# A cross-attention block and a maxout MLP on one core: all loads as nine transfers on one queue, the state read in 128x32 array tiles, layer 1 by column halves

## The chip, the cores and the metric

The kernel runs on one core of one Trainium2 chip. The metric is the device time of one execution in microseconds, the median of several runs. A profile is one such execution recorded by the hardware; its span is some 2 us shorter than the device time of the same run. Engines are named as in the profile: PE (TensorE matmul), PEld (its weight loads), DVE (VectorE), ACT (ScalarE), POOL (GpSimd), SP (the sync engine, which here only issues DMA).

## The reference

For 8 batches of 8 heads, `x` (512 x 64 per head) reads from a `state` (32 x 64 per head) and the state reads from `x`; both results go through a maxout MLP.

```python
scores = scale * x @ state.T ;  xread = softmax(scores) @ state        # 512 rows a batch
scores2 = scale * state @ x.T ; sread = softmax(scores2) @ x           # 32 rows a batch
t = concat([xread, sread])      # (8*544, 512) over all heads
out = maximum(t @ w1, t @ w2) @ w_out      # w1, w2: 512x1024, w_out: 1024x512
```

Both kernels compute max(a, b) as b + relu(a - b). So they need w1 - w2 (the "weight subtraction", into `wcat[:, :, 0:1024]`), and w2 times w_out (into `wcat[:, :, 1024:1536]`, here "the product"). They never form xread: the state is multiplied by the weights first (`u_sw`, "state times weights"), then by the attention.

## The kernel before

The parts that the change touches, with cuts marked. In the traces here each engine takes up its work in the order of the program: x of batch 0 was cast by 12.5 us in this kernel, but its transposes wait behind those of the state until 21.4.

```python
for b in range(B):                                  # state: 8 pieces of 64 KB, ACT queue
    nc.scalar.dma_start(out=s_f[32 * (b % 4):32 * (b % 4) + 32, b // 4, :]..., in_=state[b]...)
load_x(0); load_x(1)                                # two transfers of 512 KB each, SP queue
for i in range(4):                                  # weights: 8 row blocks of 512 KB, SP queue
    nc.sync.dma_start(out=w2f[:, i, :], in_=moe_w2[128 * i:128 * i + 128])
    nc.sync.dma_start(out=w1f[:, i, :], in_=moe_w1[128 * i:128 * i + 128])
...
def u_sr(b, g):                                     # state read: E^T x, whole array
    for c in range(NC):
        nc.tensor.matmul(p[:, 0:257], d["e"][:, c, 4*g:4*g+4, :]..., d["xb"][:, c, g, 0:257], ...)
    nc.vector.reciprocal(d["rr"][:, g:g + 1], p[:, 256:257])
    nc.vector.tensor_scalar(d["sr"][:, :, g, :], p[:, 0:256]..., scalar1=d["rr"][:, g:g + 1], ...)
...
cast_x(0, ("V", "A"))
states(0)                                           # state transposes, batches 0 to 3
states(1)                                           # the same for batches 4 to 7
cast_x(1)
for b in range(2):
    for u in att_units(b):                          # attention of batches 0 and 1
        u()
for i in range(4):
    w_t(i)                                          # transposes of w2; subtractions beside them
    ...
u_sw(0, 0); u_sw(0, 1)
l1(0, ...); l1(1, {})                               # layer 1 of batches 0 and 1
for i in range(4):
    w_wo(i)                                         # the product of w2 and w_out
...
l2(0, {... attention of batch 2 ...})               # from here one batch after another
```

The softmax here doesn't subtract the row's maximum and nothing guards it: scores larger than these inputs give would overflow.

## Time and profile before

| | before |
|---|---|
| device time, median (range) of 4 runs | 196.72 us (194.87 to 197.77) |
| span of the profiled run | 195.7 us |
| PE busy | 162.1 us, 83% |
| first layer 1 matmul | 48.6 us |
| layer 2 of batch 0 starts | 66.2 us |
| one batch in the steady part | 16.7 us |

The steady part is nearly pure matmul time, so a change helps either by starting it earlier or by taking PE work out of it. The lines are in the prediction. One caution on reading them: the clock column of that run says 1.00 all through, yet its transposes at 21 us are 107 ns apart and those at 68 us 56 ns. The spacing of equal instructions is the better witness of the clock; the clock record of that run is not complete.

### The profile page before, as it was taken

The numbers are of one execution on the slowest core, as the hardware profiler recorded it, in microseconds if no ns is written. First come the engines' busy times: TensorE is split into PE (matmuls) and PEld (weight loads), VectorE is DVE, ScalarE is ACT, GpSimd is POOL, SyncE is SP. The second block draws the span as 40 slices with busy tenths as digits, with TensorE's granted clock in tenths as the row PEclk, the third lists the DMA queues.
The fourth block names the chain that finished last, engine by engine and source line by source line (L and its number), as shares of the span: only waits on it lengthen the run. The fifth ranks groups of instructions, "written<-read, shape, count | busy, mean of one in ns | idle before, by whom it ended". The sixth has DMA issues, their size and how long they took to land.

```text
span 195.7 us, 2920 instructions
## 1 busy us (share of the span) xinstructions
PE 162.1 (83%) x1192; PEld 84.1 (43%) x1192; DVE 92.1 (47%) x171; ACT 71.2 (36%) x123; POOL 36.4 (19%) x48
## 2 busy tenths in 40 slices
PE   0020688646999899999999999999999999999992
PEld 0010556432344356556445544545544544474440
DVE  1120465737670236466763584475277554232510
ACT  0050324264653351344811822562280261232311
POOL 1010540940000008043260071026004000000000
PEclk9999999999999999999999999999999999999999
DMA  5999970093000000943900750390050050052222
GB/s 166 323 343 381 376 233 3 0 165 50 0 3 0 0 0 5 281 150 121 302 9 3 229 199 3 139 290 2 3 214 0 3 214 0 0 218 54 55 107 107
DMA packets 14797, 23.25 MB, mean 119 GB/s; under 512 B 2880, under 2 KB 12096, under 8 KB 13888
## 3 DMA queue, kind: packets, MB, share of 16 engines
q1 hardware_dynamic: 11568, 21.50, 32.4%
q0 software_dynamic: 1040, 1.05, 3.5%
q10 hardware_dynamic: 2176, 0.52, 1.3%
q8 instruction: 9, 0.15, 0.3%
q14 instruction: 4, 0.03, 0.1%
HBM read 15.20 MB, written 8.91 MB: 123 GB/s over the span
## 4 chain that ended last, share of the span: by engine, by line
PE 67%; DMA 9%; ACT 9%; DVE 8%; issue 3%; POOL 2%; ACTq 1%; DVEq 0%; POOLq 0%
PE ps L249 26%; PE ps L234 11%; DMA s_f<-in_state_dram 9%; PE ps L247 7%; PE ps L144 4%; PE ps L291 4%; DVE es L163 3%; PE ps L210 3%; PE ps L175 3%; DVE r L225 2%; PE ps L186 2%; ACT xt L58 2%; PE ps L285 2%; POOL a L165 2%; ACT e L162 2%
## 5 line engine op out<-in xcount | busy, mean ns | idle before, releaser
L249 PE MATMUL ps<-wo,r 128*128 128x512 bf16 x256 | 61.2, 379 | 0.8 <-DVE r L225 0.8
L249 PEld LDWEIGHTS <-r 128*128 128x128 bf16 x256 | 25.0, 98 | 32.5 <-DVE r L225 2.8
L165 POOL TENSOR_TENSOR a<-e,er 128x512 bf16<-128x512 bf16 x16 | 16.6, 1046 | 94.5 <-DVE er L164 94.5
L234 PE MATMUL ps<-aT,sw 128*128 128x512 bf16 x128 | 33.5, 388 | 0.0
L58 ACT COPY ob<-ps 128x512 f32<-128x512 f32 x16 | 9.4, 585 | 58.7 <-PE ps L249 58.7
L225 DVE TENSOR_SCALAR r<-ps 128x512 bf16<-128x512 f32 x32 | 21.6, 674 | 10.0 <-PE ps L234 9.8
L223 ACT ACTIVATE r<-ps 128x512 bf16<-128x512 f32 x32 | 19.3, 604 | 6.3 <-PE ps L234 6.3
L60 DVE CAST sw<-ps 128x512 bf16<-128x512 f32 x24 | 16.2, 679 | 9.2 <-PE ps L210 9.1
L247 PE MATMUL ps<-sw,aT 128*128 128x512 bf16 x64 | 19.2, 381 | 0.6 <-DVE sw L60 0.6
L60 DVE COPY ob<-ps 128x512 f32<-128x512 f32 x16 | 10.9, 684 | 16.7 <-PE ps L249 16.7
L110 PE MATMUL ps<-ident,s_bf 128*128 128x128 bf16 x8 | 1.2, 308 | 19.5 <-DVE s_bf L60 19.5
L58 ACT CAST sw<-ps 128x512 bf16<-128x512 f32 x24 | 14.0, 589 | 7.2 <-PE ps L210 7.2
L163 DVE TENSOR_REDUCE es<-e 128x16 f32<-128x512 bf16 x16 | 10.7, 667 | 12.3 <-ACT e L162 12.3
L234 PEld LDWEIGHTS <-sw 128*128 128x128 bf16 x128 | 11.0, 100 | 11.0 <-issue 2.9
L62 POOL CAST xb<-xf 128x1024 bf16<-128x1024 f32 x14 | 15.1, 1107 | 0.0
L210 PE MATMUL ps<-wcat,st 64*32 64x512 bf16 x192 | 10.9, 405 | 0.7 <-DVE wcat L326 0.4
L175 PE MATMUL ps<-xb,e 128*128 128x257 bf16 x64 | 11.1, 308 | 0.4 <-ACT e L162 0.4
L58 ACT COPY xt<-ps 128x1024 bf16<-128x1024 bf16 x8 | 8.1, 1010 | 8.4 <-PE ps L144 5.4
L144 PE MATMUL ps<-ident,xb 128*128 128x128 bf16 x128 | 10.8, 243 | 0.0
L144 PEld LDWEIGHTS <-xb 128*128 128x128 bf16 x128 | 9.7, 111 | 2.4
L162 ACT ACTIVATE e<-ps 128x512 bf16<-128x512 f32 x16 | 9.6, 611 | 0.4 <-PE ps L158 0.4
L60 DVE COPY xt<-ps 128x1024 bf16<-128x1024 bf16 x8 | 5.5, 688 | 8.7 <-PE ps L144 8.7
(55 smaller groups left out, 133.5 us busy)
## 6 DMA issues: line engine op xcount, KB each, us to landing
xf<-in_x_dram SPq DMA_DIRECT2D x16, 512.0 KB, 7.1
out_dram<-ob SPq DMA_DIRECT2D x7, 1024.0 KB, 5.1
w2f<-in_moe_w_dram SPq DMA_DIRECT2D x4, 512.0 KB, 6.5
w1f<-in_moe_w_dram SPq DMA_DIRECT2D x4, 512.0 KB, 7.1
wo<-in_moe_w_out_dram POOLq DMA_DIRECT2D x1, 1024.0 KB, 9.5
out_dram<-ob SPq DMA_DIRECT2D x4, 256.0 KB, 2.0
s_f<-in_state_dram ACTq DMA_DIRECT2D x8, 64.0 KB, 7.4
out_dram<-obs SPq DMA_DIRECT2D x8, 64.0 KB, 1.7
```

What stands on the lines that cost most here:

```text
L58: nc.scalar.copy(o, i)
L60: nc.vector.tensor_copy(o, i)
L144: nc.tensor.transpose(p[:, (cc * 4 + k) * 128:(cc * 4 + k + 1) * 128], d["xb"][:, c, k // 2, (k % 2) * 128:(k % 2) * 128 + 128], ident)
L163: nc.vector.tensor_reduce(d["es"][:, sl], d["e"][:, sl], axis=mybir.AxisListType.X, op=ALU.add)
L165: nc.gpsimd.tensor_mul(d["a"][:, sl], d["e"][:, sl], d["er"][:, sl].unsqueeze(3).to_broadcast([128, 2, H, Ns]))
L175: nc.tensor.matmul(p[:, 0:257], d["e"][:, c, 4 * g:4 * g + 4, :].rearrange("p i n -> p (i n)"), d["xb"][:, c, g, 0:257], start=(c == 0), s ...
L210: nc.tensor.matmul(pg[g][32 * i:32 * i + 32, :], st2[64 * g:64 * g + 64, i, b * Ns:(b + 1) * Ns], wcat[64 * g:64 * g + 64, i, ch * 512:(ch ...
L223: nc.scalar.activation(out=o, in_=p, func=ACTF.Relu)
L225: nc.vector.tensor_scalar(o, p, scalar1=0.0, scalar2=None, op0=ALU.max)
L234: nc.tensor.matmul(p, SW[b][:, g, f * 128:(f + 1) * 128], AT[b][:, g, :], start=(g == 0), stop=(g == 1))
L247: nc.tensor.matmul(p, AT[b][:, g, cs], SW[b][:, g, FF:WC], start=(g == 0), stop=False)
L249: nc.tensor.matmul(p, r[:, f, cs], wo[:, f, :], start=False, stop=(f == NF - 1))
```

## The change

Its intent: get the loads out of the way with few large transfers, in the order of need; make the state read cheaper; begin layer 1 as soon as half the weight columns are there. The core of the diff:

```diff
-    for b in range(B):
-        nc.scalar.dma_start(out=s_f[32 * (b % 4):..., b // 4, :]..., in_=state[b]...)
+    nc.sync.dma_start(out=s_f, in_=state.rearrange("b (q h) n d -> (h n) (b q) d", q=2))
     load_x(0)                      # now one transfer each
     load_x(1)
-    for i in range(4):
-        nc.sync.dma_start(out=w2f[:, i, :], in_=moe_w2[128 * i:128 * i + 128])
-        nc.sync.dma_start(out=w1f[:, i, :], in_=moe_w1[128 * i:128 * i + 128])
+    for ch in range(2):
+        cs = slice(ch * 512, (ch + 1) * 512)
+        nc.sync.dma_start(out=w2f[:, :, cs], in_=moe_w2...[:, :, cs])
+        nc.sync.dma_start(out=w1f[:, :, cs], in_=moe_w1...[:, :, cs])
+    load_x(2)
+    nc.sync.dma_start(out=wof, in_=moe_w_out...)        # was a casting DMA of POOL

-    def u_sr(b, g):                       # 2 x 4 matmuls of 257 columns, 2 evictions of 256
+    def u_sr(b):                          # 32 matmuls of 65 columns, one eviction of 128
         for c in range(NC):
+            for g in range(2):
+                for i in range(4):
+                    nc.tensor.matmul(p[32*i:32*i+32, g*65:g*65+65], d["e"][:, c, 2*i+g, :],
+                                     d["xb"][:, c, i, 1+65*g:66+65*g], ...)
     def u_srt(b):                         # 4 transposes -> 1

-    states(0); states(1); cast_x(1); att(0); att(1); w_t; subtractions
-    u_sw(0, 0); u_sw(0, 1); l1(0); l1(1); w_wo; ...; l2(0, {attention of 2})
+    warm_up(12)                           # dummy matmuls
+    states(0)
+    cast_x(0, ("V", "A", "V", "P"))       # in quarters
+    u0[0:4]; cast_x(1); u1[0], u1[1], u0[5], u1[2], u1[3], u0[4]     # 0 and 1 interleaved
+    states(1)
+    u0[6], u1[4], u1[5]; w_sub(0); u_sw(0, 0); u_sw(1, 0)
+    l1(0, first half); l1(1, first half)
+    w_sub(1); u2[0], u2[1]; u_sw(0, 1); u_sw(1, 1)
+    l1(0, second half, {u2[2], u2[3]}); l1(1, second half)
+    w_t; casts of w_out on V, A, P; u2[4:7]; w_wo; ...; l2(0, {attention of 3})
```

Here `u0[k]`, `u1[k]`, `u2[k]` are the pieces of the attention of batches 0, 1 and 2: 0 and 1 transpose x, 2 and 3 make scores and exponentials, 4 is the state read, 5 transposes the attention, 6 the state read. A "128x32 tile" is a matmul that writes 32 of the 128 output partitions; the state read's four tiles write one strip each. V, A, P name the engines DVE, ACT, POOL.

More of the change, by code (lines that the diff above doesn't have):

```diff
@@ L62, in copy, with run @@
             nc.gpsimd.tensor_copy(o, i)
-    ident = consts.tile([128, 128], BF16)
-    make_identity(nc, ident)
+    def run(*units):
+        for u in units:
+            u()
     xf_t = {}
     def load_x(b):
-        xf = xio.tile([128, 2, 4, NC * D], F32, tag="xf", name="xf")
-        xf_t[b] = xf
-        for g in range(2):
-            nc.sync.dma_start(
-                out=xf[:, g, :, :],
-                in_=x[b].rearrange("(i g) (p c) d -> g p i (c d)", g=2, c=NC)[g],
-            )
-    s_f = stage.tile([128, B // 4, DM], F32)
-    for b in range(B):
-        nc.scalar.dma_start(
-            out=s_f[32 * (b % 4):32 * (b % 4) + 32, b // 4, :].rearrange("n (h d) -> n h d", h=H),
-            in_=state[b].rearrange("h n d -> n h d"),
-        )
+        xf_t[b] = xio.tile([128, H, NC * D], F32, tag="xf", name="xf")
+        nc.sync.dma_start(out=xf_t[b], in_=x[b].rearrange("h (p c) d -> p h (c d)", c=NC))
+    s_f = stage.tile([128, 2 * B, D], F32)
+    nc.sync.dma_start(out=s_f, in_=state.rearrange("b (q h) n d -> (h n) (b q) d", q=2))
     load_x(0)
@@ L88 @@
     w1f = stage.tile([128, 4, FF], F32)
-    for i in range(4):
-        nc.sync.dma_start(out=w2f[:, i, :], in_=moe_w2[128 * i:128 * i + 128])
-        nc.sync.dma_start(out=w1f[:, i, :], in_=moe_w1[128 * i:128 * i + 128])
+    wof = stage.tile([128, NF, DM], F32)
+    for ch in range(2):
+        cs = slice(ch * 512, (ch + 1) * 512)
+        nc.sync.dma_start(out=w2f[:, :, cs], in_=moe_w2.rearrange("(i p) f -> p i f", p=128)[:, :, cs])
+        nc.sync.dma_start(out=w1f[:, :, cs], in_=moe_w1.rearrange("(i p) f -> p i f", p=128)[:, :, cs])
+    load_x(2)
+    nc.sync.dma_start(out=wof, in_=moe_w_out.rearrange("(k p) n -> p k n", p=128))
+    ident = consts.tile([128, 128], BF16)
+    warm = consts.tile([128, 512], BF16)
+    nc.gpsimd.memset(warm, 0.0)
+    make_identity(nc, ident)
+    sbd = consts.tile([128, B, 4, 2, Ns], BF16)
+    nc.vector.memset(sbd, 0.0)
     wo = consts.tile([128, NF, DM], BF16)
@@ L96, with warm_up, states @@
     w2t = stage.tile([128, 4, NF, 128], BF16)
-    s_bf = stage.tile([128, B // 4, DM], BF16)
-    s_b2 = stage.tile([128, B // 4, 4, 2, D], BF16)
-    sbd = consts.tile([128, B, 4, 2 * Ns], BF16)
-    nc.vector.memset(sbd, 0.0)
-    st2 = consts.tile([128, 4, B * Ns], BF16)
-    def states(bb):
-        copy("V", s_bf[:, bb].rearrange("p (g i d) -> p g i d", g=2, i=4),
-             s_f[:, bb, :].rearrange("p (i g d) -> p g i d", g=2, i=4))
-        p = bank(BF16)
-        for k in range(4):
-            nc.tensor.transpose(p[:, k * 128:(k + 1) * 128], s_bf[:, bb, k * 128:(k + 1) * 128], ident)
-        for jj in range(2):
-            copy("A" if jj else "V",
-                 sbd[64 * jj:64 * jj + 64, 4 * bb:4 * bb + 4, :, 32 * jj:32 * jj + 32],
-                 p[64 * jj:64 * jj + 64, 0:512].rearrange("p (k b n) -> p b k n", k=4, b=4))
-        copy("P", s_b2[:, bb], s_f[:, bb, :].rearrange("p (i g d) -> p i g d", g=2, i=4))
-        p = bank(BF16)
-        for i in range(4):
-            nc.tensor.transpose(p[:, i * 128:(i + 1) * 128], s_b2[:, bb, i].rearrange("p g d -> p (g d)"), ident)
-        copy("V", st2[:, :, 128 * bb:128 * bb + 128],
-             p[:, 0:512].rearrange("p (i t) -> p i t", i=4))
+    def warm_up(n):
+        p = bank()
+        for k in range(n):
+            nc.tensor.matmul(p, warm[:, 0:128], warm, start=(k == 0), stop=(k == n - 1))
+    s_bf = stage.tile([128, 2 * B, 2, D], BF16)
+    def states(hb):
+        qs = slice(B * hb, B * hb + B)
+        copy("V", s_bf[:, qs], s_f[:, qs].unsqueeze(2).to_broadcast([128, B, 2, D]))
+        p = bank(BF16)
+        for q in range(B):
+            nc.tensor.transpose(p[:, q * 128:(q + 1) * 128], s_bf[:, B * hb + q].rearrange("p u d -> p (u d)"), ident)
+        for g in range(2):
+            copy("A" if g else "V", sbd[64 * g:64 * g + 64, B // 2 * hb:B // 2 * hb + B // 2, :, g, :],
+                 p[64 * g:64 * g + 64].rearrange("p (b i g n) -> p g b i n", b=B // 2, i=4, g=2)[:, g])
     sread_t = consts.tile([128, 4, B * Ns], BF16)
@@ L125, with cast_x @@
     st = {}
-    def cast_x(b, engs=("P", "P")):
-        xb = xio.tile([128, NC, 2, 258], BF16, tag="xb", name="xb")
-        nc.gpsimd.memset(xb[:, :, :, 256:257], 1.0)
-        for g in range(2):
-            copy(engs[g],
-                 xb[:, :, g, 0:256].rearrange("p c (i d) -> p i c d", i=4),
-                 xf_t[b][:, g].rearrange("p i (c d) -> p i c d", c=NC))
+    def cast_x(b, engs=("P", "P", "P", "P")):
+        xb = xio.tile([128, NC, 4, 132], BF16, tag="xb", name="xb")
+        nc.gpsimd.memset(xb[:, :, :, 1:131:129], 1.0)
+        if len(engs) == 2:
+            for g in range(2):
+                copy(engs[g], xb[:, :, :, 2 + 64 * g:66 + 64 * g].rearrange("p c i d -> p i c d"),
+                     xf_t[b].rearrange("p (i g) (c d) -> p g i c d", g=2, c=NC)[:, g])
+        else:
+            for half in range(2):
+                for g in range(2):
+                    copy(engs[2 * half + g],
+                         xb[:, 2 * half:2 * half + 2, :, 2 + 64 * g:66 + 64 * g].rearrange("p c i d -> p i c d"),
+                         xf_t[b].rearrange("p (i g) (c d) -> p g i c d", g=2, c=NC)[:, g, :, 2 * half:2 * half + 2])
         st[b] = dict(xb=xb)
@@ L141, in u_xt, with u_sc @@
         for cc in range(2):
-            c = 2 * half + cc
             for k in range(4):
                 nc.tensor.transpose(p[:, (cc * 4 + k) * 128:(cc * 4 + k + 1) * 128],
-                                    d["xb"][:, c, k // 2, (k % 2) * 128:(k % 2) * 128 + 128], ident)
+                                    d["xb"][:, 2 * half + cc, k, 2:130], ident)
         copy("A" if half else "V", d["xt"][:, 2 * half:2 * half + 2].rearrange("p c k t -> p (c k t)"), p)
-    def u_sc(b, half):
+    def u_sc(b, half, mul=nc.gpsimd):
         d = st[b]
@@ L153, in u_sc @@
             d["er"] = at.tile([128, NC, H], F32, tag="er", name="er")
-            d["a"] = at.tile([128, NC, H, Ns], BF16, tag="a", name="a")
+            d["a"] = at.tile([128, 2, NC, 4, Ns], BF16, tag="a", name="a")
         p = bank()
@@ L158, in u_sc @@
                 nc.tensor.matmul(p[:, cc * 256 + k * 64:cc * 256 + k * 64 + 64],
-                                 d["xt"][:, 2 * half + cc, k, :], sbd[:, b, k, :],
+                                 d["xt"][:, 2 * half + cc, k, :], sbd[:, b, k].rearrange("p g n -> p (g n)"),
                                  start=(cc == 0 and k == 0), stop=(cc == 1 and k == 3))
@@ L164, in u_sc @@
         nc.vector.reciprocal(d["er"][:, sl], d["es"][:, sl])
-        nc.gpsimd.tensor_mul(d["a"][:, sl], d["e"][:, sl],
-                             d["er"][:, sl].unsqueeze(3).to_broadcast([128, 2, H, Ns]))
-    def u_sr(b, g):
+        mul.tensor_mul(
+            d["a"][:, :, sl].rearrange("p g c i n -> p (c i) g n"),
+            d["e"][:, sl].rearrange("p c (i g) n -> p (c i) g n", g=2),
+            d["er"][:, sl].rearrange("p c (i g) -> p (c i) g", g=2).unsqueeze(3).to_broadcast([128, 8, 2, Ns]))
+    def u_sr(b):
         d = st[b]
-        if g == 0:
-            d["sr"] = at.tile([128, 4, 2, D], BF16, tag="sr", name="sr")
-            d["rr"] = at.tile([128, 2], F32, tag="rr", name="rr")
+        d["sr"] = at.tile([128, 2, D], BF16, tag="sr", name="sr")
+        d["rr"] = at.tile([128, 2], F32, tag="rr", name="rr")
         p = bank()
         for c in range(NC):
-            nc.tensor.matmul(p[:, 0:257], d["e"][:, c, 4 * g:4 * g + 4, :].rearrange("p i n -> p (i n)"),
-                             d["xb"][:, c, g, 0:257], start=(c == 0), stop=(c == NC - 1))
-        nc.vector.reciprocal(d["rr"][:, g:g + 1], p[:, 256:257])
-        nc.vector.tensor_scalar(d["sr"][:, :, g, :], p[:, 0:256].rearrange("p (i d) -> p i d", i=4), scalar1=d["rr"][:, g:g + 1], scalar2=None, op0=ALU.mult)
+            for g in range(2):
+                for i in range(4):
+                    nc.tensor.matmul(p[32 * i:32 * i + 32, g * 65:g * 65 + 65], d["e"][:, c, 2 * i + g, :],
+                                     d["xb"][:, c, i, 1 + 65 * g:66 + 65 * g],
+                                     start=(c == 0 and g == 0), stop=(c == NC - 1 and g == 1))
+        nc.vector.reciprocal(d["rr"], p[:, 0:130:129])
+        nc.vector.tensor_mul(d["sr"], p[:, 1:129].rearrange("p (g d) -> p g d", g=2),
+                             d["rr"].unsqueeze(2).to_broadcast([128, 2, D]))
     def u_at(b):
@@ L186, in u_at, with att_units @@
                 nc.tensor.transpose(p[:, (g * NC + c) * 128:(g * NC + c + 1) * 128],
-                                    d["a"][:, c, 4 * g:4 * g + 4, :].rearrange("p i n -> p (i n)"), ident)
+                                    d["a"][:, g, c].rearrange("p i n -> p (i n)"), ident)
         copy("V", AT[b].rearrange("p g t -> p (g t)"), p)
     def u_srt(b):
-        d = st[b]
         p = bank(BF16)
-        for i in range(4):
-            nc.tensor.transpose(p[:, i * 128:(i + 1) * 128], d["sr"][:, i].rearrange("p g d -> p (g d)"), ident)
-        copy("A", sread_t[:, :, b * Ns:(b + 1) * Ns],
-             p[:, 0:640].rearrange("p (i u) -> p i u", u=160)[:, :, 0:Ns])
+        nc.tensor.transpose(p[:, 0:128], st[b]["sr"].rearrange("p g d -> p (g d)"), ident)
+        copy("A", sread_t[:, :, b * Ns:(b + 1) * Ns], p[:, 0:128].rearrange("p (i n) -> p i n", i=4))
         del st[b]
-    def att_units(b):
-        return [lambda: u_xt(b, 0), lambda: u_xt(b, 1), lambda: u_sc(b, 0), lambda: u_sc(b, 1),
-                lambda: u_sr(b, 0), lambda: u_sr(b, 1), lambda: u_at(b), lambda: u_srt(b)]
+    def att_units(b, mul=nc.gpsimd):
+        return [lambda: u_xt(b, 0), lambda: u_xt(b, 1), lambda: u_sc(b, 0, mul), lambda: u_sc(b, 1, mul),
+                lambda: u_sr(b), lambda: u_at(b), lambda: u_srt(b)]
     def u_sw(b, ch):
@@ L209, in u_sw @@
             for g in range(2):
-                nc.tensor.matmul(pg[g][32 * i:32 * i + 32, :],
-                                 st2[64 * g:64 * g + 64, i, b * Ns:(b + 1) * Ns],
+                nc.tensor.matmul(pg[g][32 * i:32 * i + 32, :], sbd[64 * g:64 * g + 64, b, i, g, :],
                                  wcat[64 * g:64 * g + 64, i, ch * 512:(ch + 1) * 512],
@@ L227, with l1 @@
     R = {}
-    def l1(b, fill):
-        r = R[b] = big.tile([128, NF, NC * 128], BF16, tag="r", name="r")
-        for f in range(NF):
+    def l1(b, fill, fs=range(NF)):
+        if fs[0] == 0:
+            R[b] = big.tile([128, NF, NC * 128], BF16, tag="r", name="r")
+        for f in fs:
             p = bank()
@@ L234, in l1 @@
                 nc.tensor.matmul(p, SW[b][:, g, f * 128:(f + 1) * 128], AT[b][:, g, :], start=(g == 0), stop=(g == 1))
-            relu(r[:, f, :], p)
-            for u in fill.get(f, ()):
-                u()
+            relu(R[b][:, f, :], p)
+            run(*fill.get(f, ()))
     def l2(b, fill):
@@ L252, in l2 @@
                 nc.sync.dma_start(out=dst[:, c:c + 1], in_=ob[:, c:c + 1])
-            for u in fill.get(NF + c, ()):
-                u()
+            run(*fill.get(NF + c, ()))
         if b < B - 1:
@@ L278, in moe_sread, with w_sub @@
                 nc.sync.dma_start(out=out[b * L + S:(b + 1) * L], in_=ob[32 * q:32 * q + 32, t, :])
+    def w_sub(ch):
+        cs = slice(ch * 512, (ch + 1) * 512)
+        nc.gpsimd.tensor_sub(wcat[:, 3, cs], w1f[:, 3, cs], w2f[:, 3, cs])
+        nc.vector.tensor_sub(wcat[:, 0:3, cs], w1f[:, 0:3, cs], w2f[:, 0:3, cs])
     def w_t(i):
-        copy("A", w2b[:, i, :], w2f[:, i, :])
         p = bank(BF16)
@@ L285, in w_t @@
             nc.tensor.transpose(p[:, f * 128:(f + 1) * 128], w2b[:, i, f * 128:(f + 1) * 128], ident)
-        copy("V" if i % 2 else "A", w2t[:, i].rearrange("p f t -> p (f t)"), p)
+        copy("A" if i % 2 else "V", w2t[:, i].rearrange("p f t -> p (f t)"), p)
     def w_wo(i):
@@ L299, in fillers @@
             u = att_units(n)
-            for slot, k in ((0, 0), (2, 1), (4, 2), (6, 3), (8, 4), (9, 5), (10, 6), (11, 7)):
+            for slot, k in ((0, 0), (2, 1), (4, 2), (6, 3), (8, 4), (10, 5), (11, 6)):
                 fill.setdefault(slot, []).append(u[k])
@@ L308, in ahead @@
         if n < B:
-            cast_x(n)
+            cast_x(n, ("P", "P"))
         if n + 1 < B:
             load_x(n + 1)
-    cast_x(0, ("V", "A"))
+    warm_up(12)
     states(0)
-    states(1)
-    cast_x(1)
-    for b in range(2):
-        for u in att_units(b):
-            u()
+    cast_x(0, ("V", "A", "V", "P"))
+    u0, u1, u2 = att_units(0, nc.vector), att_units(1), att_units(2)
+    run(*u0[0:4])
+    cast_x(1)
+    run(u1[0], u1[1], u0[5], u1[2], u1[3], u0[4])
+    states(1)
+    run(u0[6], u1[4], u1[5])
+    for i in range(4):
+        copy("P" if i == 3 else "A", w2b[:, i, 0:512], w2f[:, i, 0:512])
+    w_sub(0)
+    run(u1[6])
+    u_sw(0, 0)
+    u_sw(1, 0)
+    l1(0, {}, range(0, 4))
+    cast_x(2, ("P", "P"))
+    l1(1, {}, range(0, 4))
+    w_sub(1)
+    for i in range(4):
+        copy("P" if i == 3 else "A", w2b[:, i, 512:1024], w2f[:, i, 512:1024])
+    run(u2[0], u2[1])
+    u_sw(0, 1)
+    u_sw(1, 1)
+    l1(0, {4: u2[2:3], 5: u2[3:4]}, range(4, 8))
+    l1(1, {}, range(4, 8))
     for i in range(4):
         w_t(i)
-        if i < 3:
-            nc.vector.tensor_sub(wcat[:, i, 0:FF], w1f[:, i, :], w2f[:, i, :])
-        else:
-            nc.gpsimd.tensor_sub(wcat[:, i, 0:FF // 2], w1f[:, i, 0:FF // 2], w2f[:, i, 0:FF // 2])
-            nc.vector.tensor_sub(wcat[:, i, FF // 2:FF], w1f[:, i, FF // 2:FF], w2f[:, i, FF // 2:FF])
-    nc.gpsimd.dma_start(out=wo, in_=moe_w_out.rearrange("(k p) n -> p k n", p=128))
-    load_x(2)
-    u_sw(0, 0)
-    u_sw(0, 1)
-    l1(0, {3: [lambda: u_sw(1, 0)], 7: [lambda: u_sw(1, 1)]})
-    l1(1, {})
+    for k, e in enumerate("VAPVAPVA"):
+        copy(e, wo[:, k], wof[:, k])
+    run(*u2[4:7])
+    load_x(3)
     for i in range(4):
@@ L336 @@
     u_sw(1, 2)
-    ahead(2)
-    u = att_units(2)
-    l2(0, {8 + k // 2: u[k:k + 2] for k in range(0, 8, 2)})
     ahead(3)
     u = att_units(3)
-    l2(1, {8: u[0:2] + [lambda: u_sw(2, 0)], 9: u[2:4] + [lambda: u_sw(2, 1)], 10: u[4:6] + [lambda: u_sw(2, 2)], 11: u[6:8]})
+    l2(0, {8: u[0:1], 9: u[1:2], 10: u[2:3], 11: u[3:4]})
+    l2(1, {8: u[4:5] + [lambda: u_sw(2, 0)], 9: u[5:6] + [lambda: u_sw(2, 1)], 10: u[6:7] + [lambda: u_sw(2, 2)]})
     for b in range(2, B):
```

## The prediction

> **What bounds the kernel now.** I read the page first, for the shape of the span.
>
> ```profile
> PE 162.1 (83%) x1192; PEld 84.1 (43%) x1192; DVE 92.1 (47%) x171; ACT 71.2 (36%) x123; POOL 36.4 (19%) x48
> PE   0020688646999899999999999999999999999992
> DMA  5999970093000000943900750390050050052222
> ```
>
> A digit is 4.9 us. TensorE is at 9 from about 50 us on; until 20 us it is nearly idle while the DMA row is full; from 20 to 50 us neither is full. So there are three stages: loads, attention of heads groups 0 and 1 with the weight preparation, and a matmul-bound rest. The busy time by stretches gives the last one's reserve (one batch index per stretch, PE first):
>
> ```profile
> 20.00:37.00 17.00, 13.74 (x112) 9.88 (x112) 9.33 (x23) 5.06 (x8) 8.13 (x9) 1.00 0.49 166
> 37.00:46.50 9.50, 4.10 (x34) 3.08 (x32) 5.21 (x5) 6.06 (x7) 4.13 (x5) 1.00 0.72 110
> 90.60:107.30 16.70, 16.49 (x136) 8.26 (x134) 10.42 (x20) 6.67 (x13) 4.10 (x5) 1.00 0.39 127
> ```
>
> There PE has 0.2 us idle in 16.7: only fewer or shorter matmuls help. In the first two it waits for evictions. Next the chain that ended last, in order of time (start, us, what):
>
> ```profile
> 2.35 7.43 DMA s_f<-in_state_dram
> 9.80 10.15 DMA s_f<-in_state_dram
> 20.07 0.44 DVE s_bf L60
> ...
> 37.45 0.95 ACT w2b L58
> ...
> 47.24 0.69 DVE wcat L326
> 47.98 0.61 PE ps L210 x2
> ...
> 66.20 0.59 PE ps L247 x2
> ```
>
> The state's last piece is what lets attention start: 20.05 us, although x of batch 0 landed at 5.2. The timeline says why: the fifth load of the sync queue is issued at 5.21, when the first has landed, and the eighth of the state at 9.8. With eight loads under way a ninth waits for a landing, so state pieces queue behind x and the weights. First layer 1 matmuls start at 48.6, layer 2 of batch 0 at 66.2.
>
> **What the Trainium skill says.** (1) "TensorE: Matmul & The Clock Gate", Part 1: the array starts at half clock and gets the full one after about 3.4 us of steady work. The trace agrees: 16 transposes take 1.72 us at 21.6 (107 ns each), 0.89 at 68.5 (56 ns); the clock is half through the whole of 20 to 48 us, as TensorE stops and starts, and turns full at about 50, some 3.7 us after dense work began. (2) "DMA: Bandwidth & Descriptors", Specifications: transfers want runs of at least 512 B. The state has 256 B runs: its queue moved 0.52 MB in 1.3% of the span, 2.5 us on all engines, 205 GB/s; the sync queue 21.5 MB in 32.4%, 339 GB/s. Agrees. (3) "TensorEngine Tiling (Array Packing)", Key Properties and Restrictions: a change of tiling mode drains the array, column tiling gives up fast weight load. In the trace the eight 64x32 matmuls of a state-times-weights block take 0.34 us; a full 512-column matmul takes 0.216, so about 0.12 is drain. (4) "SBUF — State Buffer", SBUF: two separate sides: VectorE with two SBUF inputs and GpSimd can block each other. A 1024-column subtraction took 1.88 us beside a GpSimd cast, 1.22 else; the cast 2.03 for 1.03.
>
> **Part 1, loads.** Nine transfers; eight go at once, in order on one queue. By the trace bytes start at 2.3 us; state 2.5 us, then 1 MB per 2.8 to 3.0 us (350 to 375 GB/s). Seen landed, with 0.3 us for the receipt: state 5.2, x0 8.2, x1 11.2, first halves of w2 and w1 13.9 and 16.6, second 19.3 and 22.1, x2 25, w_out (2 MB, now f32) 30.5. Every transfer after x1 is wanted later than that below, so it is hidden. This takes off the 12 us between x0's and the state's being there; the second state transpose is halved too (one layout instead of two).
>
> **Part 2, the attention of 0 and 1, by hand in program order, cold clock.** Durations of before: 8 transposes 1.05, transposed copy DVE 0.69 or ACT 1.01, scores 0.61, exp 0.60, reduce 0.69, reciprocal 0.25, multiply POOL 1.05 or (estimate from the 512-column DVE subtraction, 0.68) DVE 0.65.
> - State cast 5.9, transposes 7.4, copies 7.9. Cast of x0 in quarters on three engines: 8.2 to 8.9.
> - Batch 0: transposes 8.9 to 10.9, DVE copy 10.7, ACT copy 11.95, exp 12.6 and 13.2. Then DVE alone: reduce, reciprocal, multiply twice, 12.6 to 15.7.
> - Batch 1's copy 16.4, batch 0's A^T copy 17.4; scores and exp of 1 to 18.4; its reduces and reciprocals 19.7; state read of 0 evicted 20.1; second state cast 20.8, its transposes 21.9, copies 22.4; state read of 1 23.7; A^T of 1 copied 24.85.
> - DVE subtraction of 3x512 columns (1.22 minus 0.68 over 512 columns is 1.05 ns each, so 1.75): 26.6. State times weights and eviction: 28.1, first layer 1 matmul, against 48.6. So 20.5 us are won to here. DVE, not the loads, sets this stage.
>
> **Part 3, layer 1 in halves gives part of it back.** Between the two points 48.6 and 57.5 the old kernel had layer 1 alone, with all weights ready. Now: first halves, 8 cold (0.427 each) then 8 warm matmuls, 33.4, last relu 34.1; second subtraction on DVE 35.85; transposed copy of batch 2 36.5; state times weights 37.3; second halves with scores and reduces of batch 2, DVE 3.3+1.4 us, PE to about 41.5; 32 weight transposes 43.3, their copies 44.2; w_out casts on three engines (three of 0.58 on ACT, three of 0.43 on DVE) 45.9; state read of 2 evicted after them 45.7, its transpose, then w2 times w_out from 46.0, 32 x 0.216 = 6.9, to 52.95; copy, state times the last columns, eviction: layer 2 of batch 0 at 54.8. Old: 66.2. Won: 11.4.
>
> **Part 4, the matmul-bound rest.** Batch 2's attention no longer lies in layer 2 of batch 0: 0.89 + 0.47 + 0.88 + 0.45 + 0.22 = 2.9 us of PE less. State read in tiles: eight matmuls of 257 columns (0.88 us) become 32 of 65 columns, four side by side. If columns stream side by side: 8 x 65 columns = 0.22, plus drain 0.12 to 0.24; if each goes at the 29 ns of the 64-column score matmuls (16 in 0.47): 0.93 plus drain. No row of before shows which; I take 0.85 as the middle. With three transposes fewer (0.17) that is 0.2 a batch, 1.0 for batches 3 to 7. DVE's relief there (two evictions of 0.48 and 0.16 become about 0.45 in all) is worth at most the 0.2 of idle. The rest is as before.
>
> **Sum.** 11.4 + 2.9 + 1.0 = 15.3; less 0.5 for the subtraction beside a GpSimd cast; 197.5 - 14.8 = 182.7 with the cold clock in Part 2. The twelve warm-up matmuls (1.3 to about 6.4 us) may keep it full: then transposes, scores, tiles and the first eight layer 1 matmuls on this path shrink by about 4 us: 178.7. Before, half-busy work from 20 to 46 us never released the clock, and gaps of 2 us follow the warm-up; but staying full may need less than getting there. I weigh 60 to 40: 181.
>
> **Rivals.** (a) The loads stay the bound: if one queue orders large pieces at less than 350 GB/s, or the 2 KB weight runs are slow, second halves arrive after 34 and w_out after 44 us. For it: the small pieces of before had up to 404 GB/s in 16 to 20 us. Against: that is the same queue and engines, and it would need 225 GB/s. It would give 183 to 188. (b) The tiles cost more: a weight load per tile waiting for the array to be free, 50 ns each, 1.6 us plus drain; +0.8 a batch instead of -0.2, in six or seven batches that the end depends on: 187. For it: weight loads of 128 columns last 98 ns on average without overlap. Against: eight 64x32 loads were over in 0.11 us. (c) Everything warm and tiles side by side (saves 0.5 more a batch): 175. (d) No gain, since the matmul-bound part sets the time anyway: against it, the chain runs through state load and attention until 48 us, all of it serial with the rest; I give it almost nothing.
>
> **Range and chances.** Cold 182.7, warm 178.7, tiles -2.5 to +5, scheduling by hand +-2: low 175, high 187. A slowdown needs (b) twice over plus a lost prologue. Faster by over 2% (below 193.5): 0.97; within: 0.02; slower: 0.01.
>
> **What would show it.** State landed at 5 to 6 us and x0 at 8 to 9; first layer 1 matmul at 25 to 29; DVE over 60% busy from 8 to 27; transposes at 107 ns there (cold) or 56 (warm); layer 2 of batch 0 starts at 51 to 56; PE still at 9 after; a state read of 0.4 to 1.1 us. Wrong: a DMA wait on the chain after 12 us, PE below 9 in the rest, or a period per batch above 17 us.

## The result, and the profile after

Ratios in this document are the mean time of one kernel's fast runs over that of the other's in the same rounds, so not quite the ratio of the quoted medians.

| | before | after |
|---|---|---|
| device time, median of 4 runs | 196.72 us | 181.12 us (179.51 to 181.50) |
| ratio | 1 | 0.9198, 95% interval 0.9116 to 0.9279 |
| span of the profiled run | 195.7 us | 177.7 us (the fastest of its runs) |
| first layer 1 matmul | 48.6 us | 27.0 us |
| layer 2 of batch 0 starts | 66.2 us | 54.4 us |
| one batch in the steady part | 16.7 us | 16.1 us |

The head of the page of the changed kernel, with busy times and the busy rows in 40 slices of 4.4 us:

```profile
PE 157.5 (89%) x1372; PEld 78.6 (44%) x1372; DVE 88.2 (50%) x157; ACT 71.1 (40%) x128; POOL 37.8 (21%) x52
PE   7467449599798999999999999999999999999991
DVE  2248785978305155359246644742692462323410
PEclk9955856969999999999999999999999999999998
DMA  5999999910000023077019304900500230133133
```

The first 7s and 4s of PE are the dummy matmuls. PE stays at 8 or 9 from about 49 us on, as before, but by then layer 1 of two batches and the attention of three are done. Now DVE has high digits from 13 to 44 us, with a dip at 27 to 31, and the clock row has 5s and 6s between 9 and 40 us.

Its chain of waits (start, duration, what), cut to what matters:

```profile
2.81 9.72 DMA xf<-in_x_dram
12.57 2.75 POOL xb L62 x4
...
23.50 2.00 DVE wcat L287
...
32.50 1.75 DVE wcat L287
...
43.38 1.60 DVE wo L60 x3
...
45.68 6.92 PE ps L298 x32
...
54.41 0.59 PE ps L251 x2
```

The state has left the chain. Until 12.5 us it runs through x of batch 1, then POOL's cast of it; after that through DVE, with the two weight subtractions (L287) and the casts of w_out, up to the product (L298). The later weight transfers are nowhere on it.

The stretches from the first attention to layer 1, and of one batch (busy time PE, PEld, DVE, ACT, POOL, then clock, DMA share, GB/s):

```profile
9.50:27.00 17.50, 10.41 (x170) 7.75 (x170) 12.70 (x24) 7.50 (x15) 7.92 (x11) 0.60 1.06 381
75.40:91.50 16.10, 15.89 (x154) 7.66 (x153) 8.98 (x17) 6.66 (x12) 4.27 (x5) 1.00 0.41 132
```

DVE is busy 73% of the first, at a mean clock of 0.60. In the second PE still idles only 0.2 us: the batch became shorter because it holds less PE work.

The state read on the chain, where it lies in layer 2 and nothing waits: the kernel before, then the changed one (the second lacks one record of 32):

```profile
74.19 0.88 PE ps L175 x8
```

```profile
66.72 0.36 PE ps L181 x31
```

**Where the time went.** By the two profiled runs, layer 2 of batch 0 starts 11.8 us earlier, and from there to the end it takes 123.3 instead of 129.5 us, 6.2 less. Of these 2.9 are batch 2's attention, which now lies ahead of that point, and most of the rest is 0.6 for each batch from 3 to 7. The sum, 18.0 us, is larger than the difference of the medians, 15.6, because the profiled run of before (197.87 us) was slower than the four in the table and that of the changed kernel was its fastest.

### The profile page after: what moved, and what is told of

It reads as the page before. It is cut to its first block, busy times and chain, and to the rows that moved or that the text cites. A ratio compares the mean times of both kernels' runs of the same rounds, so it can differ in the third digit from the quotient of the medians.

```text
span 177.7 us, 3246 instructions
## 1 busy us (share of the span) xinstructions
PE 157.5 (89%) x1372; PEld 78.6 (44%) x1372; DVE 88.2 (50%) x157; ACT 71.1 (40%) x128; POOL 37.8 (21%) x52
## 4 chain that ended last, share of the span: by engine, by line
PE 70%; DVE 13%; DMA 5%; ACT 4%; issue 3%; POOL 2%; SPq 1%; ACTq 0%; DVEq 0%
PE ps L253 28%; PE ps L239 13%; PE ps L251 8%; DMA xf<-in_x_dram 5%; PE ps L298 4%; DVE es L165 4%; PE ps L215 3%; PE ps L146 3%; DVE r L229 3%; PE ps L194 2%; DVE wcat L287 2%; PE ps L267 2%; PE ps L277 2%; ACT e L164 2%; POOL xb L62 2%
## 5 line engine op out<-in xcount | busy, mean ns | idle before, releaser
L239 PE MATMUL ps<-aT,sw 128*128 128x512 bf16 x128 | 35.5, 405 | 1.0 <-DVE sw L60 1.0
L167 POOL TENSOR_TENSOR a<-e,er 128x512 bf16<-128x512 bf16 x14 | 15.1, 1081 | 79.4 <-DVE er L166 79.4
L229 DVE TENSOR_SCALAR r<-ps 128x512 bf16<-128x512 f32 x32 | 21.4, 670 | 10.3 <-PE ps L239 10.2
L60 DVE CAST sw<-ps 128x512 bf16<-128x512 f32 x24 | 16.1, 683 | 17.8 <-PE ps L215 17.8
L62 POOL CAST xb<-xf 128x1024 bf16<-128x1024 f32 (+1 forms) x17 | 15.8, 958 | 14.4 <-DMA xf<-in_x_dram 14.4
L239 PEld LDWEIGHTS <-sw 128*128 128x128 bf16 x128 | 11.4, 103 | 14.1 <-issue 4.3
L146 PE MATMUL ps<-ident,xb 128*128 128x128 bf16 x128 | 11.1, 242 | 4.1 <-ACT xb L58 2.9
L215 PE MATMUL ps<-wcat,sbd 64*32 64x512 bf16 x192 | 10.1, 405 | 4.2 <-DVE wcat L287 3.9
L160 PEld LDWEIGHTS <-xt 128*128 128x128 bf16 x128 | 6.5, 108 | 4.0 <-ACT xt L58 0.7
L215 PEld LDWEIGHTS <-sbd 64*32 64x32 bf16 x192 | 2.5, 89 | 12.1 <-issue 7.7
```

The costliest lines, as they stand in the source:

```text
L60: nc.vector.tensor_copy(o, i)
L62: nc.gpsimd.tensor_copy(o, i)
L146: nc.tensor.transpose(p[:, (cc * 4 + k) * 128:(cc * 4 + k + 1) * 128], d["xb"][:, 2 * half + cc, k, 2:130], ident)
L167: mul.tensor_mul(d["a"][:, :, sl].rearrange("p g c i n -> p (c i) g n"), d["e"][:, sl].rearrange("p c (i g) n -> p (c i) g n", g=2), d["er ...
L215: nc.tensor.matmul(pg[g][32 * i:32 * i + 32, :], sbd[64 * g:64 * g + 64, b, i, g, :], wcat[64 * g:64 * g + 64, i, ch * 512:(ch + 1) * 512] ...
L229: nc.vector.tensor_scalar(o, p, scalar1=0.0, scalar2=None, op0=ALU.max)
```

## The experiments

Theory: the time came from the state's late landing and the program order that made attention wait for it, plus less PE work a batch; then DVE and the clock set the start. Rivals: the size of the transfers and the single queue themselves; the warm-up; the halves. Times are medians on their chip; the kernel before was at 198.66 us in the first call, 196.57 in the second, 197.18 in the third, so ratios are to be compared. r1 to r4 and r9 to r12 stand against the changed kernel only by way of the kernel before. They were run at other times. A run more than 1.5% above the fastest of its kernel counts as slow and is left out of the ratios; r1 and r2 have two fast runs each. Every run gave correct results.

| run | ratio to before (95%) |
|---|---|
| the changed kernel again | 0.9204 (0.9162 to 0.9245) |
| r1 changed, state read on the whole array | 0.9361 (0.9297 to 0.9426) |
| r2 changed, loads cut as before | 0.9178 (0.9126 to 0.9230) |
| r3 before, state first on the SP queue | 0.9502 (0.9462 to 0.9542) |
| r4 changed, layer 1 whole | 0.9174 (0.9137 to 0.9211) |
| r5 changed, no warm-up | 0.9231 (0.9193 to 0.9268) |
| r7 changed, dummies in gaps | 0.9227 (0.9187 to 0.9267) |
| r8 changed, second state transpose later | 0.9170 (0.9128 to 0.9211) |
| r9 changed, w_out casts on POOL | 0.9133 (0.9088 to 0.9179) |
| r12 both of r8 and r9 | 0.9069 (0.9013 to 0.9125) |
| r10 both, and dummies | 0.8954 (0.8906 to 0.9001) |
| r11 before, second state transpose later | 0.9769 (0.9717 to 0.9821) |

The slow runs may not be mere noise. Of the versions that keep the wait ahead of the product (see r7), 9 of 38 runs were slow. All four slow ones with a profile (r1, r2, r5, r8) had half clock in the product, though the fast ones of r4 and r7 had it too; of the 18 runs without that wait (r9, r12, r10) none was slow. If so, leaving them out hides part of what the wait costs. For the slow runs without a profile it is not shown.

### The state at the head of the queue (r3)

```diff
 # kernel before
-        nc.scalar.dma_start(out=s_f[32 * (b % 4):...
+        nc.sync.dma_start(out=s_f[32 * (b % 4):...
```

> The kernel before with one word changed: the eight pieces of the state go at the head of the sync queue instead of the scalar queue; no transfer is larger. My theory (order and the limit of eight under way, not size, kept the state back): all state lands by 6 to 7 us, x0 by 9 to 10, attention starts at about 9 instead of 20 and layer 1 about 10 us earlier, since attention of 0 and 1 (17 us) and weight transposes (9) then hide the weights' landing; time 186 to 188. Rival (large transfers are what count): x and weights now come later in the small pieces, attention starts after 15, time above 192.

Measured: 188.82 us against 198.66, ratio 0.9502. One word gives 5.0 of the 8.0%, with not one transfer larger. The timeline of r3 (start, duration, engine, what; L144 are the transposes of x, L247 opens layer 2):

```profile
12.35 1.91 PE L144 MATMUL ps<-ident,xb 128*128 128x128 bf16 x16
56.97 0.59 PE L247 MATMUL ps<-sw,aT 128*128 128x512 bf16 x2 [0.55 <-DVE sw L60]
```

Attention starts at 12.35 instead of 21.4, layer 2 of batch 0 at 57.0 instead of 66.2. The weights come later in the same small pieces and nobody waits for them. The theory had attention at about 9 us and a time of 186 to 188, so it came later than that; the mechanism holds. The word also frees ACT, which in the kernel before issues state pieces until 10.1 us; how much of the gain that is, no run separates.

### The program order alone (r11)

```diff
 # kernel before
     states(0)
-    states(1)
     cast_x(1)
     for b in range(2):
         for u in att_units(b):
             u()
+    states(1)
```

> The kernel before with one line moved and no load touched: the second state transpose goes behind the attention of batches 0 and 1. My theory (the program order, which puts a transpose that needs the last state piece ahead of all attention, made the load count): attention starts at 10 to 12.5 us instead of 21, and the run is 8 to 10 us faster than before, ratio 0.945 to 0.96, as with the state at the head of the queue. Rival (the small transfers hold up x and the weights as well): less than half of that, above 0.975.

Measured: 191.73 us against 197.18, ratio 0.9769. My expectation of 8 to 10 us failed; it is 2.3%, on the rival's side of the line. The timeline of r11:

```profile
13.07 1.68 PE L144 MATMUL ps<-ident,xb 128*128 128x128 bf16 x14 [0.87 <-ACT xb L58]
28.80 0.54 DVE L60 CAST s_bf<-s_f 128x512 bf16<-128x512 f32 x1
61.21 0.59 PE L247 MATMUL ps<-sw,aT 128*128 128x512 bf16 x2 [0.55 <-DVE sw L60]
```

Attention, all but two transposes, does start 8.3 us earlier, later than expected because ACT issues the state's pieces until 10.6 us and casts its half of x only from 11.97. But only 5.0 of it reach layer 2: on the chain the second state transpose, with its cast and copies, now takes 28.3 to 31.1 us, in front of the weight work. In r3 the same transposes lay before 12.35 us, where they cost some 1.2 us (x was cast by 11.1) and not 2.8. Layer 1 lost time as well: by the chain its first six matmuls take 2.77 us, in r3 1.81. So the rival's reason, small transfers that hold up x and weights, is not what the trace shows; I had forgotten the moved work itself. The lesson is narrower than my theory: the order removes the wait, the early landing also hides most of the work.

### The old cut of the loads in the new schedule (r2)

```diff
 # changed kernel
-    nc.sync.dma_start(out=s_f, in_=state...)
+    for b in range(B):
+        nc.scalar.dma_start(out=s_f[:, 2*b:2*b+2, :], in_=state[b].rearrange("(q h) n d -> (h n) q d", q=2))
-    (x in one transfer, weights in four column halves)
+    (x in two transfers, weights in eight row blocks)
```

> The changed kernel with the loads cut as before: state in eight pieces on the scalar queue, x in two halves, weights in eight row blocks on the sync queue. My theory (a ninth transfer waits for a landing, so the last state pieces and the weights' start queue behind x): the loads' gain goes: in the changed kernel only the first half of the state (all batches' pieces land one by one, the first four by 10 us) is wanted early, but its cast takes columns of four batches only, so batch 0 starts at 10 to 12 us instead of 8.9; the second state cast, at 20, waits little. The whole is 1 to 4 us slower, 182 to 185. Rival (the transfers' size and single queue are worth the whole prologue gain): 10 us slower or more, above 190.

Measured: 184.49 us against 198.66, ratio 0.9178 by its fast runs, not clearly apart from the changed kernel's 0.9204. Two of its four runs were slow ones, 186.2 and 186.3, and the profile fell on one of them. Its transposes of batch 0 start at 10.95 us (the timeline), against 9.57 in the changed kernel:

```profile
10.95 1.89 PE L147 MATMUL ps<-ident,xb 128*128 128x128 bf16 x16 [1.77 <-ACT xb L58]
```

The rival, 10 us slower, is out. The theory's 1 to 4 us don't show in the fast runs; the 1.4 us at the start of attention are there in the trace, but whether they reach the end stays open. Fewer and larger transfers are not what made the kernel faster. But r2 brings back the cut of the loads and not their lateness: six of its first eight loads are state pieces, in the kernel before four, and the last piece lands at 10.2 us instead of 19.95.

### The state read put back on the whole array (r1)

```diff
 # changed kernel
-                for i in range(4):
-                    nc.tensor.matmul(p[32*i:32*i+32, g*65:g*65+65], d["e"][:, c, 2*i+g, :], d["xb"][:, c, i, ...], ...)
+        for g in range(2):
+            for c in range(NC):
+                nc.tensor.matmul(p[:, 0:260], d["e"][:, c, 4*g:4*g+4, :]..., d["xb"][:, c, :, 1+65*g:66+65*g], ...)
     # two evictions of 256, four transposes again; scores write the heads in that order
```

> The changed kernel with the state read undone: eight matmuls of 260 columns on the whole array, two evictions, four transposes, all else as changed. My theory: the read's 0.36 us in the matmul-bound part becomes 0.88 again and three transposes (0.17) come back, so a batch takes 16.7 us instead of 16.13 and the run is 2.5 to 4 us slower than the changed kernel, 184 to 185 us; the first layer 1 matmul moves by less than 1 us. Rival (the tiles are worth nothing on the end, because the evictions that follow set the pace): within 1 us of the changed kernel, 181.

Measured: 187.62 us against 198.66, ratio 0.9361 against 0.9204: 1.7%, some 3.1 us, within what the theory said, though from two fast runs. By its trace (of a slow run) a batch takes 16.75 us, against 16.13. The groups by shape (busy us, mean ns of one) for r1, then the changed kernel:

```profile
L179 PE MATMUL ps<-xb,e 128*128 128x260 bf16 x64 | 10.0, 305 | 0.9 <-DVE r L230 0.9
L184 DVE TENSOR_SCALAR sr<-ps,rr 128x256 bf16<-128x256 f32 x16 | 7.7, 484 | 0.6
```

```profile
L181 PE MATMUL ps<-xb,e 128*32 128x65 bf16 x256 | 3.7, 202 | 0.0
L185 DVE TENSOR_TENSOR sr<-ps,rr 128x128 bf16<-128x128 f32 x8 | 2.3, 292 | 0.3
```

A matmul of a tile lasts 202 ns, but 32 of them leave PE free after 0.36 us: four run side by side in the columns. Of the products that the whole-array form computes only one in four is used (a head's exponentials with the same head's x). DVE saves 5.4 us in all as well, which is not on the steady part's path.

### Layer 1 whole (r4)

```diff
 # changed kernel
-    u_sw(0, 0); u_sw(1, 0); l1(0, first half); l1(1, first half); w_sub(1); casts of w2
-    u2[0], u2[1]; u_sw(0, 1); u_sw(1, 1); l1(0, second half, ...); l1(1, second half)
+    w_sub(1); casts of w2
+    u_sw(0, 0); u_sw(1, 0); u_sw(0, 1); u_sw(1, 1)
+    l1(0); u2[0], u2[1]; l1(1, {u2[2], u2[3]})
```

> The changed kernel with layer 1 of batches 0 and 1 over the whole width: the second weight subtraction right after the first, then all four state times weights blocks, then layer 1 of 0 and of 1. My theory (running layer 1 by halves gives time back: VectorE reaches the second subtraction only at 32.5 though its data landed at about 25): first layer 1 matmul 1 to 1.5 us later (28 to 28.5), layer 2 of batch 0 at 51.5 to 53 instead of 54.4; 1 to 3 us faster, 178 to 180. Rival (the halves hide the landing of the second halves of the weights): first layer 1 matmul 3 us later or more, and the run slower by 1 to 3 us.

Measured: 182.42 us against 198.66, ratio 0.9174, its interval overlapping the changed kernel's: neither theory. On the timeline DVE's two subtractions, back to back beside POOL's own parts, take 4.23 us instead of 2.00 and 1.75; its casts of w_out take 2.44, in the changed kernel's second profile 2.29:

```profile
24.65 4.23 DVE L287 TENSOR_TENSOR wcat<-w1f,w2f 128x1536 bf16<-128x1536 f32 x2
43.03 2.44 DVE L60 CAST wo<-wof 128x512 bf16<-128x512 f32 x3
45.93 0.23 PE L200 MATMUL ps<-ident,sr 128*128 128x128 bf16 x1 [2.80 <-DVE sr L185]
```

Layer 1 starts at 29.93 us, later than either theory had it, yet is through earlier: the transposes of w2 behind it begin at 39.43 instead of 40.85 us (second profile). PE then stands 2.8 us in front of the product, and the product takes 8.76 us instead of 7.07 (45.99 to 54.75), so that layer 2 begins at 56.58, not at 51.5 to 53. As the program stands, the halves are worth nothing clear in either direction. What whole layer 1 saves is lost at the wait treated next, and no run tried it without that wait.

### The warm-up and the clock (r5, r7)

```diff
 # r5: changed kernel
-    warm_up(12)
 # r7: changed kernel
+    warm_up(10)
     u_sw(0, 0)
 ...
+    warm_up(8)
     u_sw(0, 1)
```

> The changed kernel itself, so that the others of this call have it on the same chip in the same rounds. Expected: a ratio of 0.91 to 0.925 to the kernel before, single runs spread by 2 to 4 us, since each run meets the clock gate at another moment (the earlier runs of it had mean clocks of 0.929 to 0.95).

> The changed kernel without the twelve warm-up matmuls. In the changed kernel's trace the transposes of batch 0 at 9.6 us are 107 ns apart, so the clock had gone down again before the first of them. My theory: the warm-up matmuls buy nothing; same within 1 us, attention of batch 0 at the same times. Rival (they start the clock's later release, at 21 us): without them the clock stays half until layer 1 and the run is 1 to 3 us slower.

> The changed kernel with ten dummy matmuls ahead of the first state times weights block and eight ahead of the second one, in gaps of 2.35 and 1.6 us in which TensorE waits for the weight subtraction. In the changed kernel six matmuls after each gap run at 427 ns instead of 216. My theory (the gaps send the clock down, and on this path it counts): both layer 1 stretches run at 216 ns, 2 to 3 us less. Rival (VectorE's evictions and the relu set those stretches, or the clock's windows fall otherwise): within 1 us.

Measured in the same rounds: the changed kernel 180.72 us, r5 181.13, r7 181.05. The warm-up buys nothing that five rounds show. r7 also fails as stated, and its timeline tells why. The changed kernel (its second profile), then r7; L239 is the first half of layer 1, L200 the wait ahead of the product, L298 the product:

```profile
27.71 5.52 PE L239 MATMUL ps<-aT,sw 128*128 128x512 bf16 x16 [0.41 <-DVE sw L60]
46.68 0.23 PE L200 MATMUL ps<-ident,sr 128*128 128x128 bf16 x1 [2.95 <-DVE sr L185]
46.74 7.07 PE L298 MATMUL ps<-wo,w2t 128*128 128x512 bf16 x32
```

```profile
27.92 3.63 PE L239 MATMUL ps<-aT,sw 128*128 128x512 bf16 x16 [0.62 <-DVE sw L60]
45.11 0.23 PE L200 MATMUL ps<-ident,sr 128*128 128x128 bf16 x1 [2.96 <-DVE sr L185]
45.17 8.76 PE L298 MATMUL ps<-wo,w2t 128*128 128x512 bf16 x32
```

The dummies did bring the clock back: layer 1's half takes 3.63 instead of 5.52 us, and the product starts 1.6 us earlier. Then PE waits 2.96 us for DVE, and the product runs partly at half clock, 8.76 instead of 7.07 us. In this run the gain is given back behind a wait that I had left in.

### Work off DVE's path (r8, r9, r12, r10)

```diff
 # r8: changed kernel
-    states(1)                      # after the state read of batch 0
     ...
     for i in range(4):
         w_wo(i)
+    states(1)
 # r9: changed kernel
     (after the second casts of w2)
+    for k in range(NF):
+        copy("P", wo[:, k], wof[:, k])
     ...
-    for k, e in enumerate("VAPVAPVA"):
-        copy(e, wo[:, k], wof[:, k])
 # r12: both;  r10: both, and warm_up(7) at the two places of r7
```

> The changed kernel with the second state transpose (batches 4 to 7, first wanted at about 75 us) moved from 20.5 us to after the product of w2 and w_out. My theory (VectorE in program order sets the time from 13 to 26 us): its cast of 0.69, a wait for the transposes and a copy of 0.42 leave the path; first layer 1 matmul 1.0 to 1.6 us earlier and the run as much faster. Rival (the landing of weights or ScalarE's casts of w2 sets it): no change.

> The changed kernel with all eight casts of w_out on GpSimd, where they fit between 33 us (landing) and 38 us, instead of on three engines ahead of batch 2's state read. In the changed kernel TensorE stands 1.4 to 2.95 us there, waiting for VectorE, and after the longer gap the product of w2 and w_out took 8.4 to 9.8 us instead of 6.9. My theory (this wait and the clock drop behind it are on the path and swallow what is saved ahead of them): no gap above 0.5 us, the product at 6.9 to 7.1 us and starting at 43.5 to 44.5; the run 2 to 4 us faster than the changed kernel, ratio to before 0.90 to 0.91. Rival (w_out lands later than that, or GpSimd is slowed by VectorE and takes the wait's place): within 1 us, 0.915 to 0.925.

> Both edits: the second state transpose later and all w_out casts on GpSimd. Theory: the 1.1 us that the first edit saves ahead of layer 1 now reaches the end, since no wait follows that takes it up: 3 to 5 us faster than the changed kernel, ratio 0.895 to 0.905. Rival (something else still waits there, so that savings ahead of it vanish): the same as the casts on GpSimd alone.

> Both edits and seven dummy matmuls in each of the two gaps ahead of the state times weights blocks. Theory: layer 1's stretches at full clock, 1 to 2.5 us less than without the dummies (5.5 to 3.6 us in the earlier run), and the product's clock is not lost behind them: ratio 0.885 to 0.90. Rival (the drop only moves on): as without the dummies.

Measured: r8 180.06 us, ratio 0.9170, not clearly apart from the changed kernel's 0.9204 in the same rounds, and three of its eight runs were slow ones, 183.2 to 184.7. Layer 1 did begin 0.9 us earlier, but in the profiled run, a slow one, the product then lost the clock as in r7:

```profile
26.82 6.15 PE L239 MATMUL ps<-aT,sw 128*128 128x512 bf16 x16 [0.41 <-DVE sw L60]
46.42 0.29 PE L200 MATMUL ps<-ident,sr 128*128 128x128 bf16 x1 [2.95 <-DVE sr L185]
46.50 10.01 PE L298 MATMUL ps<-wo,w2t 128*128 128x512 bf16 x32
```

r9, 179.47 us, ratio 0.9133, takes that wait away (one record of the product is missing here and in r10):

```profile
45.49 0.23 PE L200 MATMUL ps<-ident,sr 128*128 128x128 bf16 x1
45.77 6.85 PE L298 MATMUL ps<-wo,w2t 128*128 128x512 bf16 x31
```

No gap above 0.3 us, no half clock; 0.8% less than the changed kernel, with intervals that overlap, and less than the 2 to 4 us expected, since layer 1's own stretches still ran at half clock in that run and the product still began at 45.8. With both edits (r12) 178.12 us, 0.9069, now 1.5% below the changed kernel, but short of the 0.895 to 0.905 expected, and its interval overlaps that of r9. With the dummies too (r10) 175.85 us, 0.8954, as expected:

```profile
26.43 3.63 PE L239 MATMUL ps<-aT,sw 128*128 128x512 bf16 x16 [0.62 <-DVE sw L60]
41.60 0.23 PE L200 MATMUL ps<-ident,sr 128*128 128x128 bf16 x1 [0.74 <-DVE sr L185]
41.88 6.85 PE L298 MATMUL ps<-wo,w2t 128*128 128x512 bf16 x31
```

The dummies that bought nothing alone are worth 1.3% once the wait behind them is gone. r10 is the fastest version found, 2.7% faster than the changed kernel (0.8954 over 0.9204) and 10.5% than the one before; the two ratios are from different calls, so the 2.7% is less sure than either.

## Why the prediction was right or wrong

- **What bounded the kernel, right.** The state's landing and the serial start were the cost: r3 shows it with one word. The ninth load's wait is real there, and it is the program's own: in the packed trace the loads take eight semaphores in turn, and the fifth state piece, issued at 5.01 us, waits for the semaphore of the first, which landed at 4.99. One reading was loose: at 5.2 us only the first half of x of batch 0 had landed, the second at 7.3. In the changed kernel "eight go at once" did not happen. Issuing a load of 1 MB there held the queue 0.9 to 2.7 us, the ninth went out at 14.2, and at most six were under way.
- **Part 1, the loads: order and rate right, landings early.** The state was cast from 4.9 us (5.2 predicted), x0 8.9 (8.2), x1 12.6 (11.2), x2 27.8 (25), w_out 33.2 (30.5). The bytes kept to the plan: by 30 us 9.9 MB had moved (330 GB/s), and the nine transfers have 10.0. What was too small is the 0.3 us from the last byte to the landing: counting bytes in the order of the queue it is 1.0 to 2.9 us from x0 on; why, no run tells. "Every transfer after x1 is hidden" held: none is on the chain. x1 itself is on it until 12.5 us, so the stated sign of being wrong, "a DMA wait on the chain after 12 us", came by half a microsecond; its cast by POOL follows until 15.4 us, beside DVE.
- **Part 2, DVE's program order, right from about 15 us on.** First layer 1 matmul at 27.0 and 27.7 us in two profiles (28.1 predicted). Taking one cast and one copy off DVE moved it by 0.9 (r8).
- **Part 3, the end of it right, the reason not shown.** Layer 2 of batch 0 at 54.4 and 55.6 us (54.8 predicted). That "layer 1 in halves gives part of it back" is neither shown nor refuted: whole, layer 1 ends 1.4 us earlier in the trace of r4, but the run is not clearly faster. What takes time back in both is DVE in front of the product: the casts of w_out, and in most profiles the clock lost behind them.
- **Part 4, the failed term: "I take 0.85 as the middle" for the tiled state read.** It measured 0.36 us, below the stated 0.4 to 1.1; the tiles do stream side by side. With the three transposes that is 0.6 a batch instead of 0.2, some 2 us more over five batches, and r1 shows 3.1 us at the end, with the tiles of batches 0 to 2 and the evictions. The rival of 50 ns a tile is out. "No row of before shows which" was too quick: there eight 64x32 tiles are through in 0.34 us, of which one stream of 512 columns takes 0.216, so they start at most 18 ns apart; 32 such starts would be under 0.6 us (an estimate from these two numbers).
- **"I weigh 60 to 40": the cold side was right.** At 9.6 us the transposes were 107 ns apart and the mean clock from 9.5 to 27 us 0.60. In the profiles of r7, r8, r12 and of the changed kernel again the warm-up did last to these transposes (1.26 us for 16 instead of 1.89), and layer 1 began no earlier for it (27.7 us in the last). The weighing took off 1.6 us too many; this and the tile term nearly cancel, so it is luck that 181 is closer to the measured 181.1 than its steps are.
- **What stays open.** r3 explains 5.0 of the 8.0%, the tiles 1.6 to 1.7, if the parts simply add. The remaining 1.3 or so is then the new order of the start (batch 2's attention in gaps, casts in quarters, interleaving); no run took these apart.

## What to carry to other kernels

Before making transfers larger, ask which one the first dependent instruction waits for, and where program order puts that instruction; here one word gave 5.0 of the 8.0%, and a new cut of the loads gave nothing clear. When a saving ahead of a wait doesn't reach the end, look behind it: PE stood nearly 3 us for DVE there, and the idle time often cost a second time as half clock (up to 2.9 us). So remove the last wait before the product or loop first, and judge the edits ahead of it only then; dummies worth nothing (r7) became worth 1.3% (r10).

## What the Trainium skill lacked or had wrong

- "TensorE: Matmul & The Clock Gate", the section on why this matters, warns of idle gaps over about 3 us. Here shorter gaps counted, and their length alone did not decide. In the eleven traces of the changed kernel and its variants the clock record changes only in steps of 3.41 us. In the first 58 us there are 26 steps at full clock in which PE idled 1.88 us or more, and each time the next step was at half clock; in 78 it idled at most 1.83 us, and the clock stayed full (the ends of matmuls are modelled, so the border is rough). So the gap of 2.95 us ahead of the product cost nothing in the changed kernel's second profile, where it lies across two steps (PE busy 1.92 and 1.96 of 3.41 us), and 2.9 us in r8, where one step holds most of it (busy 1.26, from 42.2 to 45.6 us, then clock 0.50). In the first profile the clock fell at 22.7 and 36.3 us while PE was busy, each time at the end of a step with 2.0 us idle.
- The same page, in "Wait — 56ns, not 53.3ns?", gives a floor of about 25 ns from start to start however few the columns. It must not be applied to column tiles: 32 matmuls of 65 columns in 128x32 tiles took 0.36 us, 11 ns each. The page's own part on packing small matmuls has tiles start about 4 ns apart, which is nearer.
- "TensorEngine Tiling (Array Packing)", Key Properties, names the drain at a change of mode without a size. Here 8 x 65 columns should stream in 0.22 us at the steady rate of 512 columns in 0.216, and took 0.36, so some 0.14 us goes to changes of mode, weight loads and issue together (an estimate; no run separates them).
